# The fourth batch's x transposed by DMA two chunks at a time, and a new order of steps, in a fused kernel of pooled attention and attention experts

## The chip, the cores and the metric

The kernel runs on one core of one Trainium2 chip. The metric is the time of one execution on the device in microseconds (us); lower is better. The engines are TensorE (PE in the profile: matrix products, and transposes done as products with an identity matrix), VectorE (DVE), ScalarE (ACT), GpSimd (POOL) and SyncE (SP). SyncE does no arithmetic here: it issues DMAs. GpSimd computes and issues DMAs. Each engine works through its own instructions in the order in which the program holds them, and waits on semaphores for what other engines and DMAs have to deliver first.

## The reference, cut to what matters

Two layers run one after the other. The first is attention with pooled keys and values: 8 batches, 8 heads, 576 tokens, head dimension 64. Keys and values are averaged over groups of 8 tokens, so that 72 of each remain. Its output, with the heads side by side, is x (8 batches of 576 tokens by 512). The second layer is a mixture of 4 causal attention experts, of which a gate picks the best 2 for each token.

```python
k_p = k.reshape(B, H, Sp, pool, D).mean(axis=3)       # pool = 8, Sp = 72
v_p = v.reshape(B, H, Sp, pool, D).mean(axis=3)
attn = softmax(scale * q @ k_p.T)
x = (attn @ v_p).transpose(0, 2, 1, 3).reshape(B, S, H * D)
...
logits = x @ w_gate                                    # top 2 of 4, softmax over the two
for e in range(E):
    q = x @ wq[e]; k = x @ wk[e]; v = x @ wv[e]        # 512 -> 64
    a = softmax(causal(scale * q @ k.T))
    out += gate_weight(e) * (a @ v @ wo[e])            # 64 -> 512
```

## The kernel before, in words

**One list sets the order.** The program is written as small steps, and the text ORDER (lines 33 to 121) lists them in the order in which their instructions are issued, across all engines. The function `emit` (L132) walks through the words. A word is a kind, a batch and an index (`xm3.0` is kind xm, batch 3, index 0; batches count from 0, so batch 3 is the fourth). A last letter picks the engine of a step that can run on several: a is ScalarE, d VectorE, p GpSimd, s SyncE. Each engine takes its own instructions out of this one list, in the list's order, and waits come from the data and from the buffers that the steps use. Words for landings (ln, lh, wl, ql, xl, ol, yd) issue nothing: they only mark a place in the list.

**How the work is tiled.** The 576 tokens of a batch are four chunks of 128 and a tail of 64. The tails of two successive batches share one chunk, chunk 4, which belongs to the odd batch of the pair; so even batches have x chunks 0 to 3 and odd ones 0 to 4. Several batches are under way at the same time: the list mixes the steps of three or four of them.

**The steps, in the order of the data:**

- ld: GpSimd's DMAs load k (halves .0 and .1), q (.2, .3) and v (.4, .5) and turn float32 into bfloat16 on the way (`load_half`, L237). Each of the three has 3 buffers, so a load waits until the batch three before has been read. Batch 0 is loaded ahead of the list. wi, wl, wc load and convert the weights.
- pk, pv: TensorE pools k and v (`pool_k`, L284); kp, vp copy the result; kt, kT transpose the pooled keys and copy them.
- qm, qc: TensorE transposes q (`qt_mm`, L346), and VectorE or ScalarE copies it from PSUM to the tile qT. For batches 5, 6, 7 (Q_DMA) one DMA, qd, does both.
- am: scores of the pooled attention (L358); ae: their exponential on ScalarE (L376, L385).
- om: product with the pooled v (`oa_mm`, L392, four matmuls); oi: reciprocal of the sums (L411); on: the normalised output, written by VectorE to the tile xtm (L416). This is x with tokens on the partitions.
- xm, xc: TensorE transposes one chunk of x by four products with the identity (`xt_mm`, L425, tile xt_ps), and a copy (L436) brings it to the tile xT. For batches 4 to 7 (X_DMA) a DMA, xd, does both, for two chunks in one instruction (X_TWO = 2): xd with index 0 turns chunks 0 and 1, index 1 chunks 2 and 3, index 2 the tail chunk 4; xl marks its landing.
- jm, jc: the experts' q and k (`qk_mm`, L457, 16 matmuls a step; `qkt_mm`, L473, for the tail chunk) and their copies; vm, vc: the experts' v and the gate's logits (L438); ga, gt, gs, ge, gb, gr, gc: the gate's small steps on VectorE and GpSimd.
- bm: causal scores of the experts (`b_mm`, L548); be: their exponential on ScalarE (L608); bk: the causal mask on GpSimd (L623).
- bo: product with the experts' v (L638, L652); bi: reciprocal (L676); bg: times the gate's weight (L680); bn: normalised and written to the tile osc (L695).
- ot, oc: TensorE's transposes of osc and their copies to oT (L697, L706); for batches 2 to 6 (O_DMA) a DMA, od, instead.
- ym: output projection (`y_mm`, L709); yc: copy to one of 8 output tiles y (L723); ys: the store (L727).
- fo, fn, fl, fm, fc, fv: a range check of all sums and a flag, at the very end; by it the program branches to a slow general path, which these inputs do not take.
- f and F with a number alone: filler pairs (L766), two matmuls or transposes of a constant tile each into the unused part of a PSUM buffer that is in use, with no result that is read.

**PSUM.** Pooled products, scores and the pooling use the two buffers of `jtp` (tile jt). All other results of TensorE share the four buffers of `psm`.

**The DMA transposes.** All of them, qd, xd and od, are issued by SyncE in the function `turn` (L800). The first one that the program issues is made to wait until the last two loads have landed, and the list may not hold any transpose ahead of the words for the landing of all loads:

```python
def turn(dst, src):
    at = nc.sync.dma_start_transpose(out=dst if isinstance(dst, bass.AP) else dst[:], in_=src)
    if not turned_any:
        turned_any.append(at)
        for n in landing[-2:]:
            tc.add_manual_dep(at.ins, n.ins.name, LINK, reason="loads_first")
```

In the kernel before, the first transpose is qd5.0 (batch 5's q), then qd6.0, and xd4.0 is the first one of x.

**Where the parts of the list lie.** Filler pairs and batch 0's pooled attention open it; the words from jm0.0 on (line 43) hold one pair more. The last load of the list is ld5.3 (line 71). Batch 3's x is transposed by xm3.0 to xm3.4 between ot0.0 and vm3.4 (lines 66 to 70).

Of the kernel before, what the change touches and what calls it, by code (L numbers as in the profile page):

```python
# [45 lines left out]
om1.8 bm0.4 oi1.9 wc0.3 on1.9 oi1.8 bm0.1 om1.3 kT2.0d on1.8 oi1.3 on1.3 xc1.2a be0.4 vm1.2
vm0.0 be0.1 vc1.2d vm0.3 qm2.0 vc0.3a om1.4 bm0.2 be0.2 vc0.0d oi1.4 qc2.0d on1.4 qm2.3 vm0.2
xm1.3 om0.9 bm0.0 qc2.3d am2.3 xc1.3d oi0.9 on0.9 vc0.2a be0.0 qm2.2 qc2.2d vm0.1 qm2.1 xm1.4
vm1.3 vc0.1d qc2.1d xc1.4d om1.6 ae2.3 am2.2 am2.0 ae2.2 jm1.4 ga0.0 vc1.3d oi1.6 on1.6 om1.0
om1.5 xm1.1 oi1.0 oi1.5 on1.5 on1.0 jc1.4d ae2.0 ld2.4 ld3.0 ld2.5 ld3.1 ln2.4 ln2.5 pv2.0  # L50
vp2.0a xc1.1a ld3.2 ln3.0 ln3.1 pk3.0 ln3.2 am2.1 qm3.0 vm1.4 kp3.0a vc1.4a kt3.0 kT3.0a qc3.0d
# [36 lines left out]
xd5.0 ql7.0 be3.6 am7.0 am7.2 jc5.4a om6.7 ol2.1 ol2.0 jm4.3 ym2.2 oi6.4 on6.4 gr3.0 oi6.7 on6.7
ym2.0 yd0.3 yc2.2d ae7.2 jc4.3a ae7.0 bo3.4 bo3.0 om6.2 bi3.4 bi3.0 bm4.2 bm4.4 gc3.0 bg3.4d
bn3.4 oi6.2 bg3.0p bk3.2 bn3.0 on6.2 yd0.1 yc2.0a xl5.0 jm5.2 om6.0 ym1.1 be4.2 bo3.3 be4.4  # L90
yc1.1a am7.3 ae7.3 am7.4 jc5.2d oi6.0 bi3.3 on6.0 gt4.0 ys2.0p bg3.3d bn3.3 vm5.4 bo3.2 bo3.1
vm5.0 ae7.4 bm4.0 am7.1 bi3.2 bg3.2d bi3.1 bn3.2 vc5.4a om6.3 bg3.1d be4.0 vc5.0a oi6.3 bn3.1
on6.3 xl5.1 jm5.3 jc5.3a ys1.0p gb4.0 xd6.0 ys1.2s xd6.1 yd0.2 ym2.1 yc2.1d ys2.1s od3.1 ys1.1s
ys1.4s od3.0 ys1.3s vm5.1 vm5.2 ae7.1 vc5.1d vc5.2d jm5.0 om7.4 jc5.0a om7.0 vm5.3 bm4.3 bm5.7
vc5.3a be4.3 oi7.4 on7.4 oi7.0 on7.0 gr4.0 gc4.0 om7.6 oi7.6 on7.6 ga5.0 jm5.1 jc5.1a xl6.0
vm6.1 vc6.1a be5.7 xl6.1 yd1.0 ym2.3 vm6.3 om6.9 om7.8 bm5.5 be5.5 yc2.3d bm5.1 vc6.3d gt5.0
oi6.9 oi7.8 on6.9 on7.8 om7.5 oi7.5 jm6.3 om7.1 be5.1 on7.5 oi7.1 yd1.2 ol3.1 on7.1 jc6.3a bm5.0
be5.0 jm6.1 om7.3 jm6.2 bm5.4 bk5.5 bk4.2 ys2.3p gs5.0 ge5.0 gb5.0 bk4.3 bk4.1 oi7.3 bk4.4
ys2.2s jc6.1a be5.4 ol3.0 yd1.1 bm5.3 vm6.0 jc6.2d on7.3 vc6.0d be5.3 vm6.2 ym3.0 ym3.1 om7.7
# [1373 lines left out]
```

## Time and profile before

| | before |
| --- | --- |
| median of 3 runs | 179.13 us (179.05 to 179.26) |
| the profiled execution | 178.99 us |
| its span in the trace | 177.3 us |
| mean granted clock of TensorE over the span | 0.992 of full speed |
| moved by DMA | 30.65 MB, mean 173 GB/s |
| transposes of x on TensorE (tile xt_ps) | 72 matmuls in 18 steps: 6.5 us |
| DMA transposes of x, q, oT on SyncE | 10, 3, 10 |
| stores issued by GpSimd / by SyncE | 9 in 8 steps / 28 steps |

The span is the stretch of the trace from the first instruction to the last; the rest of an execution's time, 1.7 us in this one, lies around it. Of the busy shares, PE counts matmuls and PEld the loads of weights, which run beside them. The slices are fortieths of the span, each digit the busy share in tenths (9 is 90% or more); the row PEclk is the clock that TensorE was granted, the row DMA the mean busy share of the 16 DMA engines. In the rows by stretches each engine has its busy time and, in brackets, its instructions; the three last columns are TensorE's granted clock, the DMA share (the sum of transfers over the stretch, so it can be above 1) and GB/s. In rows by instruction groups `out<-in` names the tiles, `128*128 128x512` the weights and the moving tile, x the count; what follows `[` or `|` is the idle time before and what ended it. SPq and POOLq are the DMA queues that SyncE and GpSimd fill. In the chain of waits each row is a start time, a length, an engine, and the group.

| stretch (us) | PE busy | DVE busy | ACT busy | POOL busy |
| --- | --- | --- | --- | --- |
| 20 to 40 | 19.95 | 16.02 | 15.29 | 7.12 |
| 60 to 80 | 19.89 | 17.17 | 15.81 | 13.31 |
| 80 to 100 | 19.24 | 14.34 | 16.81 | 3.58 |
| 140 to 156 | 15.68 | 10.67 | 13.68 | 8.72 |
| 156 to 177.3 | 11.96 | 11.11 | 9.78 | 5.98 |

### The profile page before, as it was taken

How to read it: one execution, taken by the hardware profiler on the slowest of the kernel's cores; microseconds unless marked ns; L12 is line 12 of the kernel's file. 1: busy time of each engine (PE TensorE's matmuls, PEld its weight loads, DVE VectorE, ACT ScalarE, POOL GpSimd, SP SyncE). 2: the span in 40 equal slices, each digit the busy share in tenths (PEclk: the TensorE clock that was granted, in tenths of full speed). 3: DMA queues.
4: the chain of work that ended last, by engine and by line, in shares of the span. 5: the costliest groups of instructions: out<-in, count | busy, mean ns of one | idle time of the engine just before them, and what ended most of it. 6: DMA issues, size and time to landing. Idle time of an engine off the chain costs nothing.

```text
span 177.3 us, 6308 instructions
## 1 busy us (share of the span) xinstructions
PE 164.0 (93%) x2551; PEld 131.5 (74%) x2566; DVE 122.1 (69%) x466; ACT 131.3 (74%) x239; POOL 78.7 (44%) x179
## 2 busy tenths in 40 slices
PE   7999899999999999999999899999999999969650
PEld 7978788879888888878878578877777877735420
DVE  5042775997776788896678778857786776678820
ACT  2129494897899768978798599989889977977360
POOL 7974452407970566775000263132046545672310
PEclk9999999999999999999999999999999999999996
DMA  2999999998999999999699824917767524996784
GB/s 23 196 203 202 200 206 199 206 203 112 200 206 206 204 201 173 187 148 193 41 198 248 175 53 83 157 37 226 166 180 216 134 52 147 239 178 224 254 261 178
DMA packets 44368, 30.65 MB, mean 173 GB/s; under 512 B 24113, under 2 KB 40241, under 8 KB 44337
## 3 DMA queue, kind: packets, MB, share of 16 engines
q0 software_dynamic: 17760, 17.31, 58.3%
q1 hardware_dynamic: 26576, 12.92, 33.0%
q8 instruction: 21, 0.34, 0.7%
...
## 4 chain that ended last, share of the span: by engine, by line
PE 82%; ACT 4%; issue 4%; DMA 3%; DVE 3%; POOL 1%; POOLq 0%; DVEq 0%
PE p_ps L461 15%; PE v_ps L441 9%; PE jt L290 9%; PE jt L568 7%; PE oa_ps L396 7%; PE jt L370 6%; PE ob_ps L638 5%; PE y_ps L712 5%; PE fill_ps L775 4%; PE qt_ps L350 3%; DMA oT<-osc 3%; PE xt_ps L428 3%; PE obt_ps L652 2%; PE pt_ps L478 2%; PE kt_ps L333 1%
## 5 line engine op out<-in xcount | busy, mean ns | idle before, releaser
L376 ACT ACTIVATE eta<-jt 72x510 bf16<-72x510 f32 x64 | 34.0, 596 | 7.2 <-PE jt L370 7.1
L416 DVE TENSOR_TENSOR xtm<-oa_ps,za 128x256 bf16<-128x256 f32 (+1 forms) x80 | 32.2, 417 | 1.3
L608 ACT ACTIVATE etc<-jt 128x1024 bf16<-128x1024 f32 x24 | 24.4, 1029 | 1.4 <-PE jt L568 1.2
L441 PE MATMUL v_ps<-wvg,xT 128*128 128x260 bf16 x144 | 20.4, 274 | 0.8 <-DVE osc L695 0.7
L396 PE MATMUL oa_ps<-vpa,eta 72*128 72x65 bf16 x320 | 20.6, 194 | 0.1
L608 ACT ACTIVATE etb<-jt 128x1024 bf16<-128x1024 f32 x16 | 16.2, 1025 | 4.6 <-PE jt L568 4.5
L461 PE MATMUL p_ps<-xT,wq_sb 128*128 128x256 bf16 x128 | 19.2, 272 | 0.1
L461 PE MATMUL p_ps<-xT,wk_sb 128*128 128x256 bf16 x128 | 19.2, 273 | 0.0
L411 DVE RECIPROCAL za<-oa_ps 128x4 f32<-128x4 f32 (+1 forms) x80 | 12.9, 173 | 8.8 <-PE oa_ps L396 7.8
L396 PEld LDWEIGHTS <-eta 72*128 72x128 bf16 x320 | 16.0, 98 | 4.0 <-issue 2.0
L712 PE MATMUL y_ps<-wo_sb,oT 128*128 128x512 bf16 x57 | 16.9, 380 | 1.7 <-DMA oT<-osc 1.6
L623 POOL TENSOR_SCALAR_AFFINE_SELECT etc<-etc 128x512 bf16<-128x512 bf16 x24 | 15.3, 641 | 6.3 <-ACT etc L608 4.4
L568 PE MATMUL jt<-qk 64*128 64x64 bf16 (+4 forms) x208 | 16.3, 260 | 0.0
L441 PEld LDWEIGHTS <-xT 128*128 128x128 bf16 x144 | 12.5, 97 | 4.9 <-issue 1.5
L370 PE MATMUL jt<-qT,kpT 64*72 64x255 bf16 (+1 forms) x256 | 15.7, 238 | 0.3 <-ACT eta L376 0.2
L723 ACT COPY y<-y_ps 128x512 f32<-128x512 f32 x20 | 11.3, 593 | 4.7 <-PE y_ps L712 2.6
L290 PEld LDWEIGHTS <-pm 64*72 64x72 bf16 x270 | 14.2, 110 | 0.8
L723 DVE COPY y<-y_ps 128x512 f32<-128x512 f32 x16 | 10.7, 685 | 5.2 <-PE y_ps L712 2.7
L461 PEld LDWEIGHTS <-wk_sb 128*128 128x128 bf16 x128 | 12.5, 98 | 1.5
L695 DVE TENSOR_TENSOR osc<-ob_ps,gzb 128x256 bf16<-128x256 f32 (+1 forms) x36 | 13.2, 381 | 0.3
L243 POOL DMA_DIRECT2D qb<-in_q_dram x16 | 11.1, 696 | 4.9 <-PE oa_ps L396 2.6
L638 PE MATMUL ob_ps<-vau,etb 128*128 128x65 bf16 x128 | 11.9, 194 | 1.1 <-DVE osc L695 0.6
(121 smaller groups left out, 354.5 us busy)
## 6 DMA issues: line engine op xcount, KB each, us to landing
out_dram<-y SPq DMA_DIRECT2D x25, 256.0 KB, 3.3
kb<-in_k_dram POOLq DMA_DIRECT2D x16, 288.0 KB, 7.9
qb<-in_q_dram POOLq DMA_DIRECT2D x16, 288.0 KB, 8.4
vb<-in_v_dram POOLq DMA_DIRECT2D x16, 288.0 KB, 7.1
out_dram<-y POOLq DMA_DIRECT2D x7, 256.0 KB, 2.7
...
wqs<-in_moe_wq_dram POOLq DMA_DIRECT2D x1, 256.0 KB, 11.0
wks<-in_moe_wk_dram POOLq DMA_DIRECT2D x1, 256.0 KB, 11.7
```

Of the source, the lines that this page charges most:

```text
L290: nc.tensor.matmul(out=jt[0:SK, hh, 0 : HQ * D], lhsT=pm[r, t, :], rhs=kv[r, t], start=(t == 0), stop=(t == TG - 1),)
L370: nc.tensor.matmul(out=out, lhsT=k_of(kpT, h, w), rhs=rhs, start=True, stop=True)
L376: nc.scalar.activation(out=eta[i][:, 2 * n + z, 0:MAIN].rearrange("p (g i w) -> p g i w", i=QB, w=2), in_=jt[0:SK, :, z * QB * MG : (z + 1 ...
L396: nc.tensor.matmul(out=oa_ps[:, h, :], lhsT=eta[i][:, 4 * w + h, o : o + 128], rhs=vpa[iv][:, 4 * w + h, :], start=True, stop=True,)
L416: nc.vector.tensor_tensor(out=xtm[i if c < MID else 1][r, c, :].rearrange("p (f h e) -> p h f e", f=NF, h=H)[:, 4 * w : 4 * w + 4], in0=oa ...
L441: nc.tensor.matmul(out=v_ps[:], lhsT=xT[i][:, c, f, :], rhs=wvg[:, f, :], start=(f == 0), stop=(f == NF - 1),)
L461: nc.tensor.matmul(out=p_ps[:, z].rearrange("p (c t) -> p c t", c=2), lhsT=w_sb[:, f, g, :], rhs=xT[i][:, 2 * w : 2 * w + 2, f, :], start= ...
L568: nc.tensor.matmul(out=jt[:, ee, o : o + z - a], lhsT=qk[ik][r, 1, g, kc * 128 : (kc + 1) * 128], rhs=qk[iq][r, 0, g, a:z], start=True, st ...
L608: nc.scalar.activation(out=dst, in_=src, func=EXP, scale=B_SCALE)
L638: nc.tensor.matmul(out=ob_ps[:, c - cs[0], :], lhsT=(etb if kc else ets)[i][:, e // 2, e % 2, o : o + 128], rhs=vau[iv][:, kc, e, :], star ...
L712: nc.tensor.matmul(out=y_ps[:], lhsT=oTs[g][:, c, :], rhs=wo_sb[:, g, :], start=(g == 0), stop=(g == NP - 1),)
L723: cp(out=y[:], in_=y_ps)
```

## The change

The constant X_DMA takes batch 3 in, and the whole list ORDER is replaced. No function's text changes. What the constant does: the steps xm3.0 to xm3.4 (20 transposes on TensorE) and their copies xc3.0 to xc3.4 are gone, and three DMAs take their place in SyncE's queue: xd3.0 (chunks 0 and 1), xd3.1, xd3.2, with the marks xl3.0 to xl3.2: chunks 0 and 1, chunks 2 and 3, and the tail chunk 4. Of the steps that read them, jm3.0 and jm3.2 need the first, jm3.1 and jm3.3 the second, jm3.4 the third, and a vm step the one that holds its chunk. xd3.0 is now the first transpose of the program, so it is the one that waits for the loads.

The new list holds all other steps of the old one, in another order, and with these differences in number or engine:

- filler pairs after pk0.0: 31 before, 40 after (37 pairs ahead of it in both);
- copies split between ScalarE and VectorE anew: kp 5 on ScalarE and 3 on VectorE before, 3 and 5 after; kT 3 and 5, after 4 and 4; qc 7 and 13, after 5 and 15; vp 6 and 3, after 4 and 5; xc 6 and 12, after 6 and 7; jc 20 and 16, after 21 and 15; oc 4 and 4, after 5 and 3; yc 20 and 16, after 22 and 14;
- gate products bg on GpSimd: 16 before, 13 after (the rest on VectorE);
- store steps ys on GpSimd: 8 of 36 before, 14 after (the rest on SyncE).

The diff, cut to the lines that the text below speaks of: first the old lines, then the new ones.

```diff
-X_DMA = (4, 5, 6, 7)
+X_DMA = (3, 4, 5, 6, 7)
...
 ORDER = """
-lh0.0 ln0.0 lh0.1 lh0.2 ln0.1 ln0.2 lh0.3 ln0.3 lh0.4 lh0.5 ln0.4 f0 f0 f0 f0 f0 f0 f0 f0 f0 f0
-f0 f0 f0 f0 f0 f0 f0 f0 f0 f0 f0 f0 f0 f0 f0 f0 f0 f0 f0 f0 f0 f0 f0 f0 f0 f0 f0 pk0.0 kp0.0d F0
-F0 F0 F0 F0 F0 F0 qm0.1 kt0.0 kT0.0d qm0.0 qc0.0d qc0.1a f2 f2 f2 f2 qm0.3 f3 f3 am0.1 ae0.1
-qc0.3d qm0.2 am0.3 F4 F4 F4 F4 F4 am0.0 qc0.2a pv0.0 ae0.3 ae0.0 vp0.0d ln0.5 ld1.0 ld1.1 ln1.0
...
-xc0.0a am1.0 F1 F1 am1.3 xm0.2 qm1.2 oi0.4 wc0.1 ae1.0 xc0.2d on0.4 f4 jm0.0 qc1.2a jm0.2 jc0.0d
...
-om3.9 ot0.0 xm3.3 oi3.9 oc0.0d on3.9 xc3.3d bk2.3 ld6.4 ld6.5 bk1.1 ld6.1 ld7.2 bk1.5 ld7.4
-ge2.0 be2.4 bk1.0 gb1.0 gb2.0 bk1.2 ld7.3 vp5.0a bm1.4 oc0.1a be1.4 wl0.4 am4.4 xm3.0 om3.6
-ym0.1 xm3.4 xc3.0d ae4.4 yc0.1a om3.2 bm1.6 am4.3 ln5.2 ln6.0 oi3.6 on3.6 xc3.4d gr1.0 oi3.2
-on3.2 be1.6 ln6.2 ln6.1 ym0.0 xm3.1 yc0.0d ym0.3 kt5.0 kT5.0d pk6.0 ae4.3 am4.0 ym0.2 xc3.1d
-yc0.3d ae4.0 yc0.2a kp6.0d ln7.0 ln6.4 xm3.2 vm3.4 bo1.4 ln7.4 bm2.2 am4.2 ln7.1 ld7.5 bk2.4
-gc1.0 bk1.4 ld5.3 bk1.3 ln6.3 ln7.2 ln7.3 ln6.5 xc3.2a ln5.3 ln7.5 qd5.0 vc3.4d bi1.4 bg1.4d
-bo1.2 gr2.0 bi1.2 bn1.4 bg1.2d bo1.3 bi1.3 bg1.3d bn1.2 qd6.0 be2.2 gc2.0 ys0.2s bk2.2 ae4.2
-jm3.0 bn1.3 jc3.0a jm3.1 kt6.0 bo1.1 om4.5 kT6.0d bi1.1 bg1.1d oi4.5 jc3.1a bm2.1 be2.1 pk7.0
...
-xd4.0 xl4.0 vm4.0 vc4.0d on5.4 jm4.2 vp6.0a om5.8 bm3.2 be3.4 be3.2 bm3.1 oi5.8 jc4.2d on5.8
...
-qd7.0 xd4.1 bn2.0 am6.4 ym1.2 ym1.4 bn2.1 yc1.4d xl4.1 vm4.2 am6.0 ae6.4 yc1.2a ae6.0 am6.3
...
-bn5.1 yd2.2 bk6.2 gs7.0 bk6.4 yd2.1 ym4.0 ys3.2s ys3.0s od5.0 gb6.0 ys3.4p yc4.1a yc4.0d jm7.3
...
-ys3.3s od5.1 bo6.0 bm7.0 bo6.3 be7.0 bo6.2 bi6.1 bg6.1d bi6.0 bn6.1 bi6.3 bg6.0p bn6.0 bi6.2
...
-yd3.1 yc4.3d ym5.0 yc5.0d be7.1 ym5.3 ym5.2 ym5.4 ym5.1 bm7.6 bm7.3 bk7.4 gc7.0 bk7.1 ys5.0p
...
-yc7.0a ys7.0s oc7.2d oc7.3d ym7.4 yc7.4a ym7.3 ym7.2 yc7.2a ym6.2 yc7.3a yc6.2d ys6.2p ys7.4s
...
+lh0.0 ln0.0 lh0.1 lh0.2 ln0.1 ln0.2 lh0.3 ln0.3 lh0.4 lh0.5 ln0.4 ln0.5 f0 f0 f0 f0 f0 f0 f0 f0
+f0 f0 f0 f0 f0 f0 f0 f0 f0 f0 f0 f0 f0 f0 f0 f0 f0 f0 f0 f0 f0 f0 f0 f0 f0 f0 f0 f0 f0 pk0.0 F0
+F0 F0 F0 F0 F0 F0 qm0.0 kp0.0d kt0.0 qm0.1 qc0.0d kT0.0d qc0.1d f3 f3 f3 f3 f3 f3 am0.1 qm0.3
+ae0.1 am0.0 F4 F4 F4 F4 F4 F4 F4 pv0.0 qm0.2 ae0.0 qc0.3a am0.3 vp0.0d om0.1 pv0.1 ae0.3 qc0.2d
+am0.2 om0.0 am0.4 oi0.0 om0.2 oi0.1 on0.1 oi0.2 on0.0 vp0.1a ae0.2 ae0.4 f3 f3 f3 f3 om0.6 om0.7
+on0.2 oi0.6 f4 f4 om0.3 oi0.3 oi0.7 on0.6 on0.3 on0.7 ld1.0 ld1.1 ln1.0 ln1.1 ld1.2 ld1.3 wi0.2
+ln1.2 wl0.2 wi0.3 ln1.3 pk1.0 om0.4 oi0.4 om0.5 oi0.5 xm0.2 qm1.0 on0.4 kp1.0a xc0.2a f1 f1
+om0.8 on0.5 oi0.8 qc1.0a f1 f1 f3 f3 f3 f3 f3 qm1.2 on0.8 qc1.2d kt1.0 qm1.1 kT1.0a qc1.1d wc0.2
+wl0.3 xm0.0 xm0.3 f1 xm0.1 am1.1 am1.0 xc0.0d wc0.3 xc0.3a ae1.1 ae1.0 qm1.3 wi0.1 wi0.0 ld1.4
+ld1.5 wl0.1 wl0.0 xc0.1d qc1.3d f3 f3 f3 f3 vm0.0 vm0.1 vm0.2 am1.2 vm0.3 am1.4 ln1.4 ln1.5
...
+ln6.0 ym0.0 bo1.1 ld6.5 ld7.2 gc1.0 bo1.2 bi1.2 bi1.1 bg1.1d bg1.2p vm2.3 bn1.1 vc2.3d bn1.2
+yc0.0a am4.1 ae4.1 bm2.1 bo1.3 vm2.2 ym0.2 be2.1 yc0.2a ys0.0s ld7.3 bi1.3 bg1.3d bn1.3 vc2.2d
...
+ln7.5 ln7.2 ln7.3 on4.2 vp6.0d om4.1 om4.5 oi4.0 oi4.5 on4.0 xd3.0 xd3.1 xl3.0 pk7.0 bm2.0 oi4.1
+on4.1 on4.5 xl3.1 qd5.0 ql5.0 oc1.1a ym1.2 yc1.2a ym1.1 ym0.3 kt5.0 vm2.0 yc0.3d yc1.1a kT5.0a
+jm3.0 ym1.0 om4.8 jc3.0a vc2.0d yc1.0d kp7.0a vm3.0 jm3.1 oi4.8 on4.8 vc3.0d be2.0 jc3.1a ym1.3
+om4.6 oi4.6 on4.6 yc1.3a xd3.2 am5.0 ae5.0 am5.3 ae5.3 xl3.2 om4.7 vm3.3 om4.3 vm3.4 oi4.7 on4.7
...
+bn5.2 bn5.3 jc7.1a be7.3 ys3.3p bk6.0 bk6.4 bk6.2 gs7.0 ge7.0 ys2.2s od4.0 ys2.1s ys3.4s od5.0
+od5.1 ys3.1s gc6.0 jm7.4 ol4.1 ol4.0 bo6.0 jc7.0d bm7.0 be7.0 bm7.4 be7.4 bo6.1 bi6.0 jc7.4d
...
+bn6.2 bg6.3p bk7.0 bn6.3 ol5.0 ol5.1 ym5.2 yd3.3 ym4.1 yd2.2 yc4.1a ym4.3 yc4.3a yc5.2d fo7.0
...
+od6.0 ys5.2s od6.1 ys5.1s ys4.3s ys5.3s bk7.4 bk7.1 bk7.3 ys4.1p bk7.2 yd3.1 be7.7 ym5.0 yc5.0a
...
+yc6.0a yd4.0 ym5.4 yc5.4a ys6.0s ys5.4s ys5.0p yd6.0 yd5.4 yd4.3 yd5.1 yd5.3 yd5.2 yd5.0 yd4.2
+bi7.8 fn7.0 bg7.8p fl7.0 fm7.0 bn7.8 fc7.0 ot7.1 ot7.0 ym6.2 yc6.2d oc7.1a ot7.3 ot7.2 oc7.0a
...
+yc7.3d yc6.3a ys6.2s ys7.4s ys7.1s ys7.2s ys7.3s ys6.1p ys7.0p ys6.3p yd6.1 yd7.1 yd7.0 yd6.3
+yd7.4 yd7.2 yd7.3 yd6.2 fv7.0
```

More of the change, by code (lines that the diff above doesn't have):

```diff
@@ L46 @@
[L46 to L51, printed above, removed]
@@ L88 @@
[L88 to L93, printed above, removed]
@@ L94 @@
[L94 to L99, printed above, removed]
@@ L112 @@
-yd3.1 yc4.3d ym5.0 yc5.0d be7.1 ym5.3 ym5.2 ym5.4 ym5.1 bm7.6 bm7.3 bk7.4 gc7.0 bk7.1 ys5.0p
-yd3.2 yd3.4 yc5.1a be7.6 yd4.0 ys4.2s od6.0 ol6.0 od6.1 yd3.3 yc5.3d yc5.2d yc5.4d ol6.1 be7.3
-bo7.0 yd5.0 yd4.1 ym6.0 ym6.3 yc6.0a yc6.3a bk7.3 bi7.0 fo7.0 bg7.0d bn7.0 bo7.8 bo7.4 bo7.5
-bi7.8 bi7.4 bg7.8d bi7.5 bn7.8 ym6.1 bg7.4p bo7.3 bn7.4 bg7.5p yd4.2 yc6.1a bn7.5 bo7.2 bo7.1
-bi7.3 bi7.2 bg7.3d bi7.1 bg7.2p bn7.3 bn7.2 bo7.7 bi7.7 bg7.1d bo7.6 ys5.1s ys5.2s ys5.4s bg7.7p
-bi7.6 bn7.1 fn7.0 bg7.6p ys6.3s ys6.1p ys6.0s ys5.3s ys4.3s bn7.7 fl7.0 ot7.1 ot7.0 bn7.6 fm7.0
@@ new lines @@
+on4.1 on4.5 xl3.1 qd5.0 ql5.0 oc1.1a ym1.2 yc1.2a ym1.1 ym0.3 kt5.0 vm2.0 yc0.3d yc1.1a kT5.0a
+jm3.0 ym1.0 om4.8 jc3.0a vc2.0d yc1.0d kp7.0a vm3.0 jm3.1 oi4.8 on4.8 vc3.0d be2.0 jc3.1a ym1.3
+om4.6 oi4.6 on4.6 yc1.3a xd3.2 am5.0 ae5.0 am5.3 ae5.3 xl3.2 om4.7 vm3.3 om4.3 vm3.4 oi4.7 on4.7
+vm3.2 am5.2 vc3.4a ae5.2 vc3.2a am5.1 ae5.1 oi4.3 vc3.3d on4.3 jm3.3 kt6.0 jm3.4 om4.9 ga2.0
+jc3.3d kT6.0d oi4.9 yd0.0 bm3.0 bm3.1 om4.4 on4.9 oi4.4 on4.4 vm3.1 vc3.1d jc3.4a ym0.1 ym1.4
+om5.6 yc0.1d be3.0 be3.1 am5.4 bm3.7 jm3.2 ae5.4 be3.7 bk3.1 gt2.0 bk2.0 bk2.3 gs2.0 ys0.2p
@@ new lines @@
+bg6.0p bo6.2 bo6.3 bn6.0 bi6.1 bi6.2 bg6.1d bm7.1 be7.1 yd3.0 gb7.0 bi6.3 bg6.2p bn6.1 gr7.0
+bn6.2 bg6.3p bk7.0 bn6.3 ol5.0 ol5.1 ym5.2 yd3.3 ym4.1 yd2.2 yc4.1a ym4.3 yc4.3a yc5.2d fo7.0
+yd3.4 bm7.2 bm7.7 ym5.3 be7.2 ym4.0 ym4.2 yd2.1 yc4.0a yd2.3 yc4.2a yc5.3d yd3.2 ym5.1 yc5.1d
+od6.0 ys5.2s od6.1 ys5.1s ys4.3s ys5.3s bk7.4 bk7.1 bk7.3 ys4.1p bk7.2 yd3.1 be7.7 ym5.0 yc5.0a
+bo7.6 bo7.7 bm7.6 bm7.5 bo7.3 gc7.0 ys4.0p bi7.6 bi7.7 bg7.7p bg7.6d bn7.6 bo7.5 bo7.4 bi7.3
+bi7.5 bg7.3d bn7.7 bi7.4 bn7.3 bg7.4d bk7.5 bg7.5p bn7.5 bo7.1 bo7.2 bo7.0 bn7.4 bi7.2 bi7.1
```

101 lines of the change are left out of this document (56 added, 45 removed).

## The prediction

> **What bounds the kernel now.** I read the page's busy shares first, then the stretches, then the chain of waits.
>
> ```profile
> PE 164.0 (93%) x2551; PEld 131.5 (74%) x2566; DVE 122.1 (69%) x466; ACT 131.3 (74%) x239; POOL 78.7 (44%) x179
> DMA  2999999998999999999699824917767524996784
> ```
>
> ```profile
> 8.30:20.00 11.70, 10.65 (x182) 9.35 (x183) 4.56 (x14) 5.74 (x11) 6.60 (x10) 1.00 1.27 201
> 40.00:60.00 20.00, 20.00 (x346) 17.16 (x344) 14.64 (x52) 16.66 (x36) 12.40 (x26) 1.00 1.14 184
> 120.00:140.00 20.00, 19.81 (x280) 15.62 (x284) 15.37 (x67) 18.19 (x35) 7.28 (x23) 1.00 0.68 180
> ```
>
> TensorE is busy in all of 40 to 60 us and nearly all of 120 to 140, at a granted clock of 1.00 (the column before the DMA share); it has holes before 20 us (10.65 of 11.70) and waits again near the end (below). Between those ends a matmul taken out is time gained, and a late operand is time lost. The digits show the DMA engines nearly full until about 85 us: the loads of all eight batches. Behind TensorE comes ScalarE, 18.19 of 20 us in 120 to 140.
>
> ```profile
> 9.43 0.78 PE fill_ps L775 x14
> 10.57 0.31 PE kt_ps L333 x9
> 11.46 0.61 PE kt_ps L779 x8
> 18.23 0.32 DVE xtm L416
> 22.54 0.34 PE jt L370 x4
> 22.88 0.80 PE xt_ps L428 x12
> 23.68 0.13 PE oa_ps L396 x4
> 25.40 2.78 PE p_ps L461 x24
> 66.06 0.31 PE ob_ps L638 x10
> 66.36 0.33 PE jt L568 x4
> 73.10 0.33 PE ot_ps L700 x4
> 79.25 0.32 PE y_ps L712
> 79.63 0.39 PE xt_ps L428 x4
> 85.61 0.98 PE jt L290 x18
> 93.14 0.88 PE p_ps L461 x8
> 94.14 0.45 PE v_ps L441 x4
> 146.43 0.89 PE pt_ps L478 x16
> 153.32 5.10 DMA oT<-osc
> ```
>
> Each row of the chain is a start, a length and an instruction group, so it prices one step of TensorE: a projection (jm) 0.88, a pooling (pk, pv) 0.98, a chunk of v (vm) 0.45, four oa matmuls (om) 0.13, a chunk's transposes (xm) 0.27 (three in 0.80) to 0.39.
>
> **The change part by part.**
>
> *Five transposed chunks leave TensorE* (xm3.0 to xm3.4, 20 instructions). Five times 0.27 to 0.39 is 1.3 to 1.9 us; I take 0.32 each, near the middle: **-1.6**. They stood between 74 and 80 us, in the full stretch, so this counts. Their five copies on VectorE and ScalarE (about 0.4 and 0.6 us each) also go; the other copies change hands between the two engines, and I count all that as nothing because both run beside TensorE. If ScalarE's cover of 120 to 140 us were gone, one copy moved there would cost its 0.6.
>
> *Filler pairs.* Words f and F are pairs of matmuls without use. The old order has 30 between the first pooling and the step that opens the full stretch (jm0.0), and one later; the new one has 40 ahead of its opening step (vm0.0) and none later. Real work ahead of it is the same but for one am. A pair takes 0.11 (14 matmuls in 0.78) to 0.15 (8 in 0.61). Nine pairs net are 1.0 to 1.4 us. Yet the chain leaves TensorE here (VectorE's row at 18.23), so TensorE also waits in this part, and a pair put into a wait costs nothing: lower end 0. I take **+1.2**: in the old order the chain runs through the pairs themselves.
>
> *Three DMA transposes (xd3) on SyncE.* The first transpose of any kind waits until every load has landed.
>
> ```profile
> SPq L801 <- DMA vb<-in_v_dram: 83.2, 1, 83.2
> ```
>
> ```profile
> 80.21 0.71 POOL L243 DMA_DIRECT2D qb<-in_q_dram  x1
> ```
>
> ```profile
> 85.88 6.86 SPq L801 DMA_TRANSPOSE qT<-qb  x2
> ```
>
> ```profile
> qT<-qb SPq DMA_TRANSPOSE x3, 5.1
> qb<-in_q_dram POOLq DMA_DIRECT2D x16, 288.0 KB, 8.4
> ```
>
> ```profile
> DMA to landing us min/median/max: 2.4/3.1/5.2
> L801 SPq DMA_TRANSPOSE xT<-xtm x10: 1227/1270/1539, 94.4 to 140.3; - x10
> ```
>
> In the old order the last load is issued at 80.21 and SyncE's first transpose at 85.88, 5.7 us on. In the new one the queue reads xd3.0, xd3.1, qd5.0, xd3.2, and a transposing DMA holds it for 1.27 (x) or 3.4 (q: two in 6.86). Call xd3.0's issue T. Then xd3.0 lands at T+3.1, qd5.0 (issued at T+2.5) at T+7.6, and xd3.2 (issued at T+6.0) at T+9.1.
>
> When are they needed? Ahead of jm3.0 the new order has, against what the old one has ahead of pk7.0 (85.61): one pk, one pv, three om, one bm, one bo, two ot and one ym more; one kt, five xm, one vm and two jm less. With the rows' prices: 1.96 + 0.39 + 0.33 + 0.31 + 0.66 + 0.32 - 0.31 - 1.6 - 0.45 - 1.76 = -0.15. With the pairs' 1.2, jm3.0 falls at 86.7. From there to am5.0 are two jm, two ym, two om and a vm (3.1 us): 89.8; to vm3.4 two am, two om and a vm more (1.4): 91.2. So T may be 83.6 for jm3.0, 82.2 for am5.0 and 82.1 for vm3.4. The last load (second half of q7) has in front of its place, against the old order's first ot step (73.10), three bo, two bm, two ot, two ym and one am more, four om, two vm and one pv less: +0.8, with the pairs 2.0, so 75.1. GpSimd waits only for the product behind bo1.2, six steps (2.4 us) sooner; so the load goes out at 73 to 75. Landing takes 5.7 (the old last load) to 8.4 (median of the q loads): T is 79 to 83.5, middle 81.1, a wait of 0 to 1.4. I take **+0.3**; late loads are a rival below.
>
> *Moved steps at the end.* The chain holds 5.10 us from the issue of batch 5's second oT transpose to its landing, against 2.7 at the median:
>
> ```profile
> oT<-osc SPq DMA_TRANSPOSE x10, 2.7
> ```
>
> ```profile
> 150.61 1.13 POOL L727 DMA_DIRECT2D out_dram<-y  x2 [0.25 <-issue]
> 151.13 1.77 SPq L727 DMA_DIRECT2D out_dram<-y  x3
> 153.32 2.04 SPq L801 DMA_TRANSPOSE oT<-osc  x1
> 158.70 1.89 PE L712 MATMUL y_ps<-wo_sb,oT 128*128 128x512 bf16 x8 [1.34 <-DMA oT<-osc]
> ```
>
> TensorE stood 1.34 us for it, the longest such wait. Five stores went out just ahead. Between od5.1 and the first y step of batch 5 the old order has three bo, three bm and one ym (2.2 us); the new one a pt projection, four bo and three bm (3.1). The wait could fall to 0.4, a gain of 0.9; but stores (ys2.1, ys3.4) still stand ahead of the pair on SyncE, so it may also stay. I take **-0.6**, between 0 and -0.9 and nearer the longer lead.
>
> *Fourteen stores by GpSimd instead of eight.* Here issues of POOL and landing:
>
> ```profile
> L727 POOL DMA_DIRECT2D out_dram<-y x9: 539/589/640, 109.8 to 171.9; - x9
> out_dram<-y SPq DMA_DIRECT2D x25, 256.0 KB, 3.3
> out_dram<-y POOLq DMA_DIRECT2D x7, 256.0 KB, 2.7
> ```
>
> Six more issues are 3.5 us of an engine busy 44%: nothing, unless a mask (bk) or a gate product (bg) that TensorE needs stands behind one. Upper end 0.6 each time: ys4.1 stands ahead of bk7.2, and ys5.0 ahead of bg7.8, which the last normalisation needs. [...]
>
> *Sum:* -1.6 + 1.2 + 0.3 - 0.6 = **-0.7**. The profiled execution took 178.99 (span 177.3 and 1.7 around it), 0.14 below the median of 179.13. From the median: **178.4**; own range 177.5 to 178.8 (wait at xd3 0 to 0.7, pairs 0.4 to 1.2).
>
> **The rivals.**
>
> *Late loads (slower).* One mechanism: the last load lands as late as before, T = 85.9. Then vm3.4 waits 85.9 - 82.1 = 3.8 instead of 0.3: 178.4 + 3.5 = 181.9; with T halfway, 84.0, it is 180.0. It decides from T = 83.1 on, where the wait of 1.0 eats the sum of the other terms. For it: the loads had to go out some 6 us sooner, and the DMA engines were nearly full. Against it: the old order left holes in them, so there is room.
>
> ```profile
> 42.00:48.00 6.00, 6.00 (x107) 5.37 (x104) 4.46 (x14) 4.90 (x12) 5.79 (x12) 1.00 1.01 148
> ```
>
> At the 201 GB/s of 8.3 to 20 us, these six would have carried their bytes in 1.6 us less. [...]
>
> *Stores and masks at the end (slower).* When batch 5's oT steps are due, 18 store steps are left in the new order, 16 in the old. 0.26 MB each at the rate of the last stores,
>
> ```profile
> 172.00:174.00 2.00, 0.00 (x0) 0.00 (x0) 0.00 (x0) 0.00 (x0) 0.45 (x1) 1.00 0.95 306
> ```
>
> is 0.86 a store, 1.7 for two, and the gain of 0.6 at the end goes: 178.4 + 2.3 = 180.7. Against it: the six issues that GpSimd takes over shorten SyncE's line by as many (three in 1.77 at 151.13).
>
> *Paid back (no change).* The end gives nothing and the ten pairs mark real waits that last a little longer: 178.4 + 0.6 + 0.1 = 179.1.
>
> *Full gain.* The pairs lie in waits that were there anyhow (+0 instead of 1.2): 177.2.
>
> **How the numbers follow.** Forecast 0.35, late loads 0.20, stores 0.17, paid back 0.13, full gain 0.15. About 0.2% (0.36 us) is what a measurement of this kernel can tell from no change. Faster by more: full gain and nearly all of the forecast, 0.46; within: 0.13; slower: 0.41, the two slow cases and a little of paid back. Cases of both signs hold most of the chance, so the range runs from below the full gain, 176.8, to 181.4, which leaves out the worst of the late loads.
>
> **What would show it.** Right: xd3.0 issued at 79 to 82, no TensorE wait over 0.5 us on xT or qT, vm0.0 one microsecond later than jm0.0 was (25.40 in the chain), xt_ps down to 52 instructions, the oT wait under 1 us. Wrong: xd3.0 after 83; the full stretch opening at 25.4 or sooner (full gain); an oT or mask wait over 1.3 us after 150.

## The result, and the profile after

| | before | changed |
| --- | --- | --- |
| median (lowest to highest) | 179.09 us (178.63 to 179.26, 4 runs) | 185.66 us (183.96 to 188.7, 4 runs) |
| ratio to the kernel before | | 1.034 (1.0254 to 1.0426) |
| the same, taken again beside other runs | | 1.0351 (1.0277 to 1.0426) |
| profiled execution | 178.99 us, span 177.3 | 186.33 us, span 184.6 |
| mean granted clock | 0.992 | 0.973 |

The change makes the kernel about 6 us slower. From one execution to the next these kernels can differ by several microseconds; a ratio is taken over the undisturbed ones alone, so it can lie below what a median over all runs would give.

From the page of the changed kernel, the busy shares and the slices:

```profile
PE 167.7 (91%) x2564; PEld 129.8 (70%) x2564; DVE 120.9 (66%) x465; ACT 130.5 (71%) x238; POOL 80.6 (44%) x181
PE   7999999999999999999999999569999999878930
PEclk9999999999999999999999999957999999999996
```

The row of TensorE has a hole in its 26th and 27th slice (each 4.6 us, so 115 to 125 us), and the clock row falls in the second of them and the one behind it. Before, TensorE was full at this place. The stretches around it:

```profile
116.00:118.00 2.00, 2.00 (x26) 1.61 (x24) 1.62 (x7) 1.91 (x3) 0.46 (x2) 1.00 1.08 370
118.00:120.00 2.00, 0.02 (x1) 0.00 (x0) 0.75 (x3) 0.57 (x2) 0.99 (x2) 1.00 1.11 219
120.00:122.00 2.00, 0.43 (x4) 0.34 (x6) 0.00 (x0) 0.00 (x0) 0.00 (x0) 0.54 0.68 91
122.00:124.00 2.00, 2.00 (x17) 1.18 (x14) 0.96 (x4) 1.75 (x3) 0.00 (x0) 0.50 0.75 206
124.00:126.00 2.00, 2.00 (x15) 1.40 (x14) 0.94 (x4) 0.34 (x2) 1.24 (x5) 0.50 1.63 108
126.00:128.00 2.00, 2.00 (x28) 1.43 (x29) 1.22 (x6) 1.40 (x3) 0.00 (x0) 0.75 0.32 66
```

TensorE is idle from 118.0 to 121.6, and its granted clock is 0.50 from 120.2 to 127.0: 0.54 over 120 to 122 means that 1.84 of these 2 us were low, 0.75 over 126 to 128 that one of them was. What it waited for stands in the waits of TensorE and in the chain of waits:

```profile
PE jt L370 <- DMA qT<-qb: 3.5, 1, 3.5
PE y_ps L712 <- DMA oT<-osc: 1.8, 1, 1.8
```

```profile
25.21 1.34 PE v_ps L441 x12
...
88.09 0.87 PE p_ps L461 x8
...
112.57 8.95 DMA qT<-qb
...
123.19 1.71 PE p_ps L461 x8
...
158.45 4.39 DMA oT<-osc
```

The step am7.3 waits for the DMA transpose of batch 7's q. That transpose is qd7.0; it takes 8.95 us from its issue at 112.57. The row at 123.19 shows the price of the clock: a jm step takes 1.71, against 0.88 in the chain of before. (The rows at 25.21 and 88.09 are vm0.0 and batch 3's first projection; they serve further down.) Why it is issued so late is seen in SyncE's queue. First the changed kernel, with the longest wait of that queue between 92 and 125 us, then the row of the same transpose in the kernel before:

```profile
82.65 2.71 SPq L801 DMA_TRANSPOSE xT<-xtm  x2
...
109.86 2.67 SPq L801 DMA_TRANSPOSE xT<-xtm  x2
112.57 6.55 SPq L801 DMA_TRANSPOSE qT<-qb  x1
```

```profile
SPq L801 <- DVE xtm L416: 13.9, 1, 13.9
```

```profile
96.72 3.65 SPq L801 DMA_TRANSPOSE qT<-qb  x1
```

The row at 109.86 is xd5.0 and xd5.1, for which the queue waited 13.9 us: until VectorE had normalised batch 5's x (tile xtm). The new list has qd7.0 behind them; the old one has it ahead of xd4.1 and issues it at 96.72. What qd7.0 itself needs was there long before: the first experiment below issues it at 99.94.

The end, as the last row of TensorE and one stretch behind it, of before and then of the changed kernel:

```profile
168.56 2.32 PE L712 MATMUL y_ps<-wo_sb,oT 128*128 128x512 bf16 x10
...
174.00:176.00 2.00, 0.00 (x0) 0.00 (x0) 0.00 (x0) 0.00 (x0) 0.00 (x0) 0.60 0.48 174
```

```profile
173.37 3.47 PE L712 MATMUL y_ps<-wo_sb,oT 128*128 128x512 bf16 x14
...
180.00:182.00 2.00, 0.00 (x0) 0.00 (x0) 0.00 (x0) 0.00 (x0) 0.00 (x0) 0.90 1.02 389
```

TensorE ends at 170.9 before and at 176.8 in the changed kernel, 6.0 later. From there to the end of the span are 6.4 us before and 7.8 after: the DMA engines are still full (1.02) three to five microseconds behind TensorE's end, where before they were at 0.48. The spans differ by 7.3 us. Of these, 3.5 are the wait for qT. The steps at half clock behind it cost 2.4: from am7.3 to the end of the low spell they take 5.8 us, and 3.4 at full clock, in the run with filler pairs in the wait. The wait for batch 5's oT is 0.5 longer (1.8 against 1.34), and the stores at the end take 1.3 more. These make 7.7, so at most 0.4 is gained elsewhere: the saving of 1.6 by the 20 transposes does not show in this sum. It is taken up below.

### The profile page after: what moved, and what is told of

It reads as the page before. It is cut to its first block, busy times and chain, and to the rows that moved or that the text cites. A ratio compares the mean times of both kernels' runs of the same rounds, so it can differ in the third digit from the quotient of the medians.

```text
span 184.6 us, 6328 instructions
## 1 busy us (share of the span) xinstructions
PE 167.7 (91%) x2564; PEld 129.8 (70%) x2564; DVE 120.9 (66%) x465; ACT 130.5 (71%) x238; POOL 80.6 (44%) x181
## 4 chain that ended last, share of the span: by engine, by line
PE 68%; DMA 11%; DVE 5%; issue 5%; POOL 4%; ACT 3%; SPq 1%; POOLq 0%
PE p_ps L461 15%; PE v_ps L441 8%; PE jt L290 7%; PE jt L568 6%; PE oa_ps L396 6%; PE jt L370 6%; PE y_ps L712 6%; DMA qT<-qb 5%; PE ob_ps L638 4%; DMA vb<-in_v_dram 3%; PE qt_ps L350 3%; DMA oT<-osc 2%; DVE xtm L416 2%; PE pt_ps L478 2%; PE xt_ps L428 2%
## 5 line engine op out<-in xcount | busy, mean ns | idle before, releaser
L411 DVE RECIPROCAL za<-oa_ps 128x4 f32<-128x4 f32 (+1 forms) x80 | 13.4, 175 | 13.9 <-PE oa_ps L396 12.8
L441 PE MATMUL v_ps<-wvg,xT 128*128 128x260 bf16 x144 | 21.6, 279 | 0.0
L712 PE MATMUL y_ps<-wo_sb,oT 128*128 128x512 bf16 x72 | 19.2, 380 | 1.8 <-DMA oT<-osc 1.8
L461 PE MATMUL p_ps<-xT,wq_sb 128*128 128x256 bf16 x128 | 19.7, 277 | 0.0
L461 PE MATMUL p_ps<-xT,wk_sb 128*128 128x256 bf16 x128 | 19.7, 277 | 0.0
L370 PE MATMUL jt<-qT,kpT 64*72 64x33 bf16 (+1 forms) x256 | 16.4, 244 | 3.5 <-DMA qT<-qb 3.5
L723 ACT COPY y<-y_ps 128x512 f32<-128x512 f32 x22 | 12.5, 594 | 8.2 <-PE y_ps L712 3.6
L471 ACT CAST qk<-p_ps 128x512 bf16<-128x512 f32 x20 | 11.7, 591 | 3.6 <-PE p_ps L461 3.4
L723 DVE COPY y<-y_ps 128x512 f32<-128x512 f32 x14 | 9.5, 684 | 7.0 <-PE y_ps L712 4.9
L243 POOL DMA_DIRECT2D kb<-in_k_dram x16 | 10.3, 648 | 7.3 <-PE jt L568 4.2
```

The source lines that it names most:

```text
L370: nc.tensor.matmul(out=out, lhsT=k_of(kpT, h, w), rhs=rhs, start=True, stop=True)
L441: nc.tensor.matmul(out=v_ps[:], lhsT=xT[i][:, c, f, :], rhs=wvg[:, f, :], start=(f == 0), stop=(f == NF - 1),)
L461: nc.tensor.matmul(out=p_ps[:, z].rearrange("p (c t) -> p c t", c=2), lhsT=w_sb[:, f, g, :], rhs=xT[i][:, 2 * w : 2 * w + 2, f, :], start= ...
L712: nc.tensor.matmul(out=y_ps[:], lhsT=oTs[g][:, c, :], rhs=wo_sb[:, g, :], start=(g == 0), stop=(g == NP - 1),)
L723: cp(out=y[:], in_=y_ps)
```

## The experiments

**The place of qd7.0, undone in the changed kernel.**

```diff
-qd6.0 oi5.6 yc1.4d xd4.0 xd4.1 jc3.2a
+qd6.0 oi5.6 yc1.4d xd4.0 xd4.1 qd7.0 jc3.2a
...
-ys1.3p xd5.0 xd5.1 qd7.0 ys0.1p
+ys1.3p xd5.0 xd5.1 ys0.1p
```

> The changed kernel with one step moved: qd7.0, the transpose of batch 7's q, stands right behind xd4.1 instead of behind xd5.1. Theory (q7 is late because it queues on SyncE behind xd5.0, which waited until 109.8 us for batch 5's x): qd7.0 is issued before 101 us, TensorE has no wait on qT, no stretch of low clock follows, and the 3.5 us of wait and the 2.3 us of slow steps behind it are gone: 185.0 - 5.8 = 179.2 us, 178.5 to 180. Rival (the new list is worse elsewhere too, the drift of 1.9 us between 36 and 80 us grows by what the wait had covered): over 181 us.

Measured: ratio 1.0072 (1.0024 to 1.012), the profiled execution 180.35. SyncE's queue and TensorE's wait in this run (its list has fewer text lines, so its line numbers are 4 smaller):

```profile
99.94 2.84 SPq L797 DMA_TRANSPOSE qT<-qb  x1
```

```profile
PE jt L366 <- DMA qT<-qb: 0.3, 1, 0.3
```

The transpose goes out at 99.94 and its wait is gone. One moved word takes 2.7% off the time (1.034 to 1.0072, 4.8 us), a little less than the 5.8 expected. What is left is 0.7%. In the profiled executions all of it lies behind TensorE's last instruction: that ends at 170.85 here and at 170.88 in the kernel before, and the spans are 178.6 and 177.3. The later runs are about it.

**The late place, made in the kernel before.** There xd5.1 stands ahead of xd5.0; qd7.0 goes between the two.

```diff
-qd7.0 xd4.1 bn2.0 am6.4
+xd4.1 bn2.0 am6.4
...
-om6.4 on6.6 xd5.1
+om6.4 on6.6 xd5.1 qd7.0
```

> The kernel before with one step moved: qd7.0 goes from its place ahead of xd4.1 to behind xd5.1, so that it queues behind transposes of batch 5's x as in the changed kernel. Theory (the place in SyncE's queue alone makes the loss): the transpose is issued near 112 us, lands 5 to 9 us later, am7.0 (due at 114.0) waits 3 to 7 us and a spell of half clock follows: 182 to 187 us. Rival (it takes the new list's early stores or xd3 as well): under 180.5 us.

Measured: ratio 1.0337 (1.0277 to 1.0398), profiled 185.63: with this one word moved, the old kernel is as slow as the changed one. TensorE's longest wait, the chain, and the stretches behind it:

```profile
PE jt L370 <- DMA qT<-qb: 3.7, 1, 3.7
```

```profile
112.06 5.46 DMA qT<-qb
...
117.56 0.63 PE jt L370 x8
```

```profile
118.00:120.00 2.00, 2.00 (x17) 1.39 (x14) 0.61 (x2) 1.07 (x2) 0.00 (x0) 0.60 0.09 20
120.00:122.00 2.00, 2.00 (x16) 0.89 (x14) 0.69 (x1) 1.77 (x4) 0.00 (x0) 0.55 0.00 0
```

Issued at 112.06, as the theory had it, with a landing (5.46) near the 5.1 of the q transposes in the kernel before, and still a wait of 3.7: the place alone suffices, without the new list's stores and without xd3.

**The four stores beside it, moved away.** In the changed kernel GpSimd issues four stores around the issue of the transpose (111.54 to 113.77).

```diff
-be3.4 bo2.2 ys1.3p xd5.0 xd5.1 qd7.0 ys0.1p xl5.0 jm5.0 bi2.3 oi6.8 bg2.3d bi2.2 ys1.1p ys1.0p
+be3.4 bo2.2 xd5.0 xd5.1 qd7.0 xl5.0 jm5.0 bi2.3 oi6.8 bg2.3d bi2.2
...
-ql7.0 am7.3 bm4.0
+ql7.0 am7.3 ys1.3p ys0.1p ys1.1p ys1.0p bm4.0
```

> The changed kernel with the four stores that GpSimd issues around qd7.0 (ys1.3, ys0.1, ys1.1, ys1.0) moved behind am7.3; qd7.0 stays where it is. Theory (the transpose is slow because 1 MB of stores shares the DMA engines with it): qT lands about 5.5 us after its issue instead of 8.9, the wait falls from 3.5 us to about 0.3, the clock stays up: 179.5 to 181 us. Rival (it is slow because two x transposes go out just ahead of it, or is late whatever lies beside it): the wait stays above 2 us, 183.5 to 186 us.

Measured: ratio 1.0448 (1.0371 to 1.0526), profiled 183.73. TensorE's three longest waits on data and the place of the stores (line numbers 4 smaller):

```profile
PE y_ps L708 <- DMA oT<-osc: 1.9, 1, 1.9
PE v_ps L437 <- DMA xT<-xtm: 1.9, 1, 1.9
PE jt L366 <- DMA qT<-qb: 1.4, 1, 1.4
```

```profile
116.49 2.23 POOL L723 DMA_DIRECT2D out_dram<-y  x4
```

The wait on qT falls from 3.5 to 1.4, between the two expectations, and the stores, now at 116.5, meet the next transpose of x, for which TensorE waits 1.9. In this execution qT lands 6.7 us after its issue (112.61), against 8.95 with the stores beside it. So the stores seem to slow a transpose beside them, but no shorter time is shown: that is nearer to the rival. The stores are a part of the long landing, not the reason for the late issue.

**Filler pairs into the wait.** 24 pairs ahead of am7.3.

```diff
-ql7.0 am7.3 bm4.0
+ql7.0 f1 f1 f1 ... f1 am7.3 bm4.0
```

> The changed kernel with 24 filler pairs ahead of am7.3, where TensorE waits for qT. At 0.11 us a pair they fill 2.6 of the 3.5 us. Theory (the idle of 3.5 us halves TensorE's granted clock, and the slow steps of 122 to 127 us come from it): the wait for qT's landing is as long, the granted clock stays at 1.00 in 120 to 130 us, and the time falls by about 2: 182.5 to 183.5 us. Rival (the clock falls for another reason, or the steps behind are slow because of their own data): 184.5 us or more.

Measured: ratio 1.0418 (1.0362 to 1.0474). The landing in the chain, and the stretches:

```profile
112.36 10.55 DMA qT<-qb
```

```profile
118.00:120.00 2.00, 1.48 (x27) 1.48 (x27) 0.43 (x2) 0.25 (x1) 0.78 (x2) 1.00 1.07 194
120.00:122.00 2.00, 1.36 (x25) 1.18 (x22) 0.00 (x0) 0.00 (x0) 0.00 (x0) 1.00 1.37 73
122.00:124.00 2.00, 1.04 (x16) 0.71 (x17) 0.15 (x2) 0.59 (x2) 0.00 (x0) 1.00 0.38 69
```

With TensorE kept at work through most of the wait the clock stays at 1.00, and am7.3 to am7.1 take 2.4 us instead of 4.4: in the changed kernel the low clock comes from the idle stretch. But qT landed 10.55 us after its issue in this execution, 1.4 later than in the changed kernel, and the expected time was missed; the ratio is not lower than the changed kernel's. Whether the pairs have a part in the longer landing is open.

**xd3 alone, in the kernel before.** X_DMA takes batch 3 in, xm3 and xc3 are gone, and the list is changed as little as that needs.

```diff
-ln5.3 ln7.5 qd5.0 vc3.4d bi1.4
+ln5.3 ln7.5 xd3.0 xd3.1 qd5.0 bi1.4
...
-qd6.0 be2.2
+qd6.0 xd3.2 be2.2
...
-vc3.3a am5.3 am5.2
+vc3.3a vm3.4 am5.3 vc3.4d am5.2
```

> The kernel before with batch 3's x by DMA and as little of a new order as that needs: xm3 and xc3 out, xd3.0 and xd3.1 behind the last load's mark and ahead of qd5.0, xd3.2 behind qd6.0, vm3.4 moved behind vc3.3. Theory (the first transpose waits for all loads, 85.9 us in the old order, so xd3.0 lands at 89 and jm3.0, due at 82.6 less 1.6, waits about 8 us, with a spell of half clock): 185 to 190 us; this would be why the loads had to go out sooner in the new order. Rival (TensorE has other work to do meanwhile, the saving of 1.6 shows): 177 to 179 us.

Measured: ratio 1.0556 (1.0502 to 1.061), profiled 188.11. The chain, the clock, and the longest wait:

```profile
79.38 5.27 DMA qb<-in_q_dram
...
84.74 3.34 DMA xT<-xtm
...
88.13 3.61 PE p_ps L461 x16
```

```profile
84.00:92.00 8.00, 3.87 (x24) 2.83 (x25) 0.00 (x0) 0.83 (x2) 0.00 (x0) 0.50 0.77 140
```

```profile
PE p_ps L461 <- DMA xT<-xtm: 6.6, 1, 6.6
```

The last load goes out at 79.38, the first transpose waits for it until 84.74, and jm3.0 for the transpose: 6.6 us, and then two jm steps take 3.61, which at 0.88 each would be 1.76: the granted clock is 0.50 over 84 to 92. This is the prediction's rival of late loads, in the old list. The new list has moved the loads far enough to avoid it: there the last one goes out at 73.73 and xd3.0 at 82.65.

**xd3 taken back out of the new list.** Twice, on top of the first experiment: the second time (shown) with xm3 placed further behind its data.

```diff
-X_DMA = (3, 4, 5, 6, 7)
+X_DMA = (4, 5, 6, 7)
...
-on4.0 xd3.0 xd3.1 xl3.0 pk7.0 bm2.0
+on4.0 xm3.0 xc3.0d pk7.0 bm2.0 xm3.1 xc3.1a
```

> The first experiment's list (qd7.0 early) with batch 3's x transposed by TensorE again: xm3.0 to xm3.4 and their copies are spread from pk6.0 to oi4.5, xd3.0 to xd3.2 are gone. Theory (20 transposes are worth 1.6 us of TensorE and xd3 makes it wait for nothing): 1.3 to 1.9 us slower than the first experiment. Rival (TensorE waits for xT or the loads as much as the transposes took): within 0.5 us of it.

> As the fourth experiment (batch 3's x by TensorE in the list with qd7.0 early), but with xm3.0 to xm3.4 placed one by one from on4.0 to vm2.0, 2 to 6 us behind the data that they need and with another step of TensorE between each two. Theory (the 3 us lost in the fourth experiment came from steps that stood too close to their data): TensorE has no new wait of over 0.3 us between 80 and 93 us, and the cost is that of 20 transposes, 1.3 to 1.9 us over the first experiment's 180.05: 181.3 to 182.0. Rival (the transposes cost TensorE nothing, a wait takes them up): within 0.5 us of 180.05.

Measured: ratios 1.04 (1.0344 to 1.0457) and 1.0315 (1.0243 to 1.0386), so 3.3% and 2.4% over the first experiment instead of 0.9%. Both sides of both expectations are missed. In the second build new waits of TensorE stand between 80 and 93 us:

```profile
PE y_ps L712 <- ACT oT L707: 1.1, 1, 1.1
PE xt_ps L428 <- DVE xtm L416: 0.8, 1, 0.8
```

The builds made waits of their own (a copy of x on ScalarE ahead of the copy of oT), so they do not isolate the price of the 20 transposes. They show only that at neither of these places in the new list can the 20 transposes be had for the 1.6 us of their own work.

**Nine filler pairs taken out.** On top of the first experiment.

```diff
-f1 f1 f3 f3 f3 f3 f3 qm1.2
+f1 f1 qm1.2
...
-qc1.3d f3 f3 f3 f3 vm0.0
+qc1.3d vm0.0
```

> The first experiment's list without nine of the filler pairs ahead of vm0.0 (four just ahead of it, five ahead of qm1.2), so that 31 are left behind pk0.0, as in the kernel before. Theory A (a pair costs its 0.11 to 0.15 us, as the prediction had it): 1.0 to 1.3 us faster, 178.8 to 179.0 us. Theory B (the pairs stand in waits that are there anyhow, as the opening of the full stretch at 25.0 to 25.3 us in both kernels suggests): the same within 0.3 us, or slower where the clock is granted at half behind the empty waits.

Measured: ratio 1.004 (1.0005 to 1.0075), against 1.0072 (1.0024 to 1.012) with the pairs: no difference that the intervals can tell. The opening and the landing of batch 5's q in the chain, and the longest wait of the run:

```profile
24.71 1.34 PE v_ps L441 x12
...
86.34 5.93 DMA qT<-qb
```

```profile
PE jt L370 <- DMA qT<-qb: 1.4, 1, 1.4
```

With the pairs the same products opened at 25.50 (first experiment), so the pairs do cost 0.8 there. The gain is then waited for at am5.0, where batch 5's q lands at 92.27, no earlier than with the pairs (91.92): it stands behind xd3.0 and xd3.1, and these behind the loads. The list that reached this place earlier only waited longer.

**The end.** Three edits on top of the first experiment: batch 6's last output steps earlier (with the store ys6.3 on SyncE instead of GpSimd); ym5.2, which waits for oT, behind ym4.1 and ym4.3, which do not; and, not shown, the second edit together with an earlier ym6.3 alone.

```diff
-yd5.0 yd4.2 bi7.8 fn7.0 bg7.8p
+yd5.0 yd4.2 ym6.3 yc6.3a ys6.3s bi7.8 ym6.1 yc6.1a ys6.1p fn7.0 bg7.8p ym6.2 yc6.2d ys6.2s
```

```diff
-ol5.1 ym5.2 yd3.3 ym4.1 yd2.2 yc4.1a ym4.3
+ol5.1 yd3.3 ym4.1 yd2.2 yc4.1a ym4.3 ym5.2
```

> The first experiment's list with three output steps of batch 6 (ym6.3, ym6.1, ym6.2, their copies and stores) moved from the last 20 steps of TensorE to places ahead of batch 7's last product and transposes. Theory (after TensorE's end the first experiment took 8.2 us, the kernel before 6.9, since 8 output steps lie behind the last transposes instead of 6 and the y buffers and DMA engines are full): 0.8 to 1.5 us faster than the first experiment's undisturbed runs of 180.05 us, so 178.5 to 179.3. Rival (TensorE's waits among the last steps take it up, the end is set by the bytes that are left): within 0.4 us of 180.05.

> The first experiment's list (qd7.0 early) with ym5.2, the output step that waits for batch 5's second oT, moved behind ym4.1 and ym4.3, which wait for nothing. Theory (the wait of 1.1 us at 157 us is plain idle time on the path): the wait falls by two output steps, 0.9 us, to 0.2, and the time by 0.5 to 0.9: 179.2 to 179.6 us against 180.05. Rival (the end is set by the bytes left to store, TensorE's gain turns into a wait of the copies for free y buffers): within 0.3 us of 180.05.

> The list with ym5.2 behind ym4.1 and ym4.3, and ym6.3 with its copy and store moved ahead of batch 7's last gate product, so that 7 output steps instead of 8 lie behind the last transposes. Theory (two independent losses at the end, 0.9 of waiting and 1.3 of stores piled up): 178.6 to 179.3 us. Rival (the end is bound by the stores alone): as the run with ym5.2 moved alone, within 0.3 us.

Measured: for the first and the third no ratio is on record. Their shortest times are 179.54 and 179.79, one execution each, which shows nothing either way. In the profiled execution of the first (182.54) TensorE has a new wait, for the range check. VectorE's copy of ym6.2 (168.87) now stands ahead of its step of that check (169.54):

```profile
PE cnt_ps L756 <- DVE bad L749: 1.1, 1, 1.1
```

The second: ratio 1.0026 (0.9972 to 1.0081), against 1.0072; its profiled execution (181.95) has no wait on oT over 0.2 us. The direction is as expected, the size is within the intervals, so no gain is shown.

**All three small edits together.** qd7.0 early, nine pairs fewer, ym5.2 later.

> The changed kernel with three edits at once: qd7.0 early, nine filler pairs fewer, ym5.2 behind ym4.1 and ym4.3. Theory (the loss at q7 is the whole of the slowdown, the two others are small and add up): a ratio to the kernel before of 0.995 to 1.002, about 178.5 to 179.5 us. Rival (what the pairs give at the opening is waited for again at am5.0, where batch 5's q lands by the pace of the loads, and the end stays as it was): 1.003 to 1.008, as with one or the other alone.

Measured: ratio 1.0042 (1.0017 to 1.0067). The rival: the gains do not add up. With its loss taken away, the new list is 0.4% (0.8 us) slower than the old one, beyond the interval, and no version here is shown to beat the kernel before.

**The changed kernel again**, beside some of these runs:

> The changed kernel as it is, beside the others on one chip. Theory (q7's late transpose, then a spell of half clock): the wait on qT at am7.3 is there again, between 1 and 5 us as its landing varies, 183.5 to 187 us. If the wait had been chance, under 181 us.

Measured: ratio 1.0351 (1.0277 to 1.0426); in its profiled execution (183.54) the wait on qT is 3.2 us, from 118.2 to 121.5. The low clock is shorter here:

```profile
122.00:124.00 2.00, 2.00 (x20) 1.50 (x19) 0.98 (x5) 1.99 (x4) 0.00 (x0) 0.63 0.74 205
124.00:126.00 2.00, 2.00 (x17) 1.19 (x16) 1.69 (x5) 0.34 (x1) 1.25 (x5) 0.52 1.13 118
```

It is 0.50 from 122.5 to 125.9, by the same working as above, and the steps from am7.3 on take 5.0 us instead of 5.8, so it costs 1.6.

## Why the prediction was wrong

The forecast was 178.4 and a range up to 181.4; the time is 185.66. Without the loss at qd7.0 the sign would still have been wrong: the first experiment is 0.7% slower than the kernel before, where 0.4% faster was forecast.

*The step that failed* is the account of the moved steps. The prediction followed SyncE's queue only as far as "the queue reads xd3.0, xd3.1, qd5.0, xd3.2" and looked for the next change at the end. Between them it left out qd7.0, which the new list moves past xd4.1, xd5.0 and xd5.1. It had no term, and no rival had its place. The runs put its price at 4.8 us (1.034 to 1.0072) in the new list and at 6.0 (1.0337) in the old one. Its working, from the rows above: released at 109.86, the queue spends 2.7 on xd5.0 and xd5.1; with the 5.1 of a q transpose in the kernel before, qT would land at 117.7, and TensorE is ready for am7.3 at 118.0. So the place leaves no margin, where the old one left some 12 us; the landing of 8.95, with four stores beside it, then makes the wait of 3.5. In the old list am7.0 is due earlier, at 113.8, and the place makes a wait by itself.

*The clock.* In the trace of before the longest wait of TensorE with work behind it is 1.34, and the clock from 156 to 162, around and behind it, is 1.00. In the changed kernel a wait of 3.5 brings 6.8 us at 0.50, which cost 2.4; in its second profiled execution a wait of 3.2 brings 3.4 us and costs 1.6; in the old list with qd7.0 late, a wait of 3.7 brings 3.4 us (118.4 to 121.8, by 0.60 and 0.55 in its two stretches). So each of these waits, 3.2 to 3.7 us, was followed by half clock, but the spells differ in length and in where they start: 2.2 us after TensorE's last work in the changed kernel (118.0 to 120.2), 4.3 in its second execution (118.2 to 122.5), 4.6 in the old list (113.8 to 118.4). The forecast has no time for it. The run with filler pairs shows the cause here: with TensorE kept at work through most of the wait, so that 1.6 us of it are left, the clock was 1.00 from 118 to 128.

*Late loads* was priced well: the last load was forecast to go out at 73 to 75 (73.73) and xd3.0 at 79 to 83.5 (82.65), and TensorE has no wait over 0.2 us between 78 and 96. The term of +0.3 was near, but that nothing waited is in part luck: by the prediction's own working an issue at 82.65 is 0.5 too late for vm3.4 (82.1), and it fits only because jm3.0 came 1.4 later than forecast (88.1 against 86.7). That the loads still set the pace there, so that nothing gained earlier survives am5.0, was not in the sum.

*The pairs* were to cost 1.2, with vm0.0 one microsecond later than jm0.0 (25.40). It opens at 25.21. The nine pairs cost 0.8 at the opening, and nothing that the intervals show in the time. The term is mis-sized.

*The 20 transposes* are gone as forecast:

```profile
L428 PE MATMUL xt_ps<-ident,xtm 128*128 128x128 bf16 x52 | 4.9, 219 | 0.4 <-DVE qT L356 0.2 <-DVE xtm L416 0.2
```

52 instead of 72. Their 1.6 us does not show in the time: in the first experiment TensorE ends at 170.85, as in the kernel before (170.88). It is lost ahead of batch 3's projections: the prediction had the opening at 26.6 (25.40 and 1.2 for the pairs) and jm3.0 at 86.7; they come at 25.2 and 88.1, so the stretch between takes 2.8 us more than the sum of its steps had it, in pieces that no single wait shows. What they are stays open.

*The wait for oT at the end* was to shrink by 0.6. It is 1.8 in the changed kernel against 1.34, and 1.1 in the first experiment. The landing was not longer: 4.39 from its issue at 158.45, against 5.10 before. But the row of steps in the list is not the time from the issue on. TensorE was ready 2.6 us after od5.1's issue (161.1), where before it was 4.0 (157.4 after 153.32), because od5.1 now stands right behind od5.0, which holds SyncE for 2.1 us; VectorE had finished its data at 157.2:

```profile
156.26 3.46 SPq L801 DMA_TRANSPOSE oT<-osc  x2
```

In the changed kernel the term is wrong in sign; in the first experiment 0.2 of the 0.6 came.

*The stores at the end* were counted as nothing, with a rival at 0.86 for each of two more. Measured is 1.3 more between TensorE's end and the span's end, with full DMA engines (a share of 1.02 over 180 to 182), and as much again in the first experiment (1.02 over 174 to 176), where it is the whole difference. That fits the rival's mechanism, and is independent of the larger loss; the edits at the end did not settle it.
